# Query products cut into steps of two and three matmuls, and the order behind the state product drawn anew

## The chip, the core and the metric

The kernel runs on one NeuronCore of a Trainium2 chip. The metric is the device time of one execution in microseconds (us); less is better. Five engines work from queues of their own, each strictly in the order in which its instructions were issued: TensorE (PE: matmuls, transposes as matmuls, and its weight loads, PEld), VectorE (DVE), ScalarE (ACT), GpSimd (POOL) and SyncE (SP, which only issues transfers here). Semaphores carry the waits between them.

## The reference

The kernel computes a transformer block on 2048 tokens of 640 features: linear attention with 32 heads of 20 features and softmax feature maps, then a two-layer SiLU network of 1728 hidden units, each behind a layer norm and with a residual.

```python
qkv = layernorm(x) @ wqkv;  q, k, v = heads(qkv)        # 32 heads of 20
pq, pk = q @ w_phi[h], k @ w_phi[h]
phi_q = concat(softmax(pq), softmax(-pq));  phi_k likewise
kv = phi_k.T @ v;  z = phi_k.sum(tokens)                # the state, per head
o  = (phi_q @ kv) / (phi_q @ z + 1e-6)
h  = x + o @ wo
out = h + silu(layernorm(h) @ w1) @ w2
```

## The kernel before

The 2048 tokens are 16 tiles of 128 (number t in what follows). The order of all instructions is written out by hand: a string `ORDER` holds words such as `dp.1@2`, and a loop calls the function `op_dp(1)` with PSUM bank 2. PSUM has eight banks of 128 x 512 fp32, and the digits behind `@` say which bank, or the first of which banks, the step writes. The loop stands in a manual schedule, so that each engine gets its instructions in the order of the words; only the waits between engines (a bank that is still read, a tile that isn't yet written) are put in by the framework.

Start. `lx`, `lk`, `lv`, `lo`, `l1`, `l2`, `lh` load x, the key and value weights, the output weights and the two network weights. `wm` are matmuls of constants on PE, of 512, 256 or 128 columns. `wt.c` transposes the key weights chunk by chunk, `wc.c` copies the chunk out, `fk.c` multiplies it with the block-diagonal w_phi (`ph` builds that on DVE) and `fc.c` copies the folded weights out; `gk`, `gc` do the same for the query weights. `st`, `rs` and `xn.t` normalise x; `xt`/`xc` (on PE) or `xd` (a transposing transfer) transpose it.

Keys and values. `kp.t` and `vp.t` are ten matmuls of 320 columns each, `ke.t` takes the two exponentials on ACT, `kr.t` the softmax sums and their reciprocals on DVE, `kn.t` scales the exponentials (L411 on POOL, L415 on DVE; the letter behind it says which of the 64 rows of 20 go to POOL: `p` all, `b` 32, `q` 48), `vc.t` copies the values out. `cc.t` adds tile t into the state, which lies in bank 7. `kc` and `km` (ACT, then DVE) bring the finished state into the form that the next stage needs.

Queries and attention. `qp.g.i` is the query product for token group g (four tiles) and feature part i (L455): parts 0 and 1 are two banks with five matmuls of 512 columns each, part 2 one bank with five. `qe.g.i` takes the exponentials with two activations on ACT (L465). `dp.t` multiplies the queries of tile t with the state (L490): forty small matmuls into four banks. `dw.t` (L508, L509, L511, L514) combines the two halves on DVE and so empties the four banks; `dr.t` takes the reciprocal, `do.t` divides (on POOL, or on DVE with `v`), `td.t` is a transposing transfer and `op.t` the output projection, ten matmuls of 320 columns (L552). `oa.t` adds it to x on DVE.

Network. `sq`, `sr`, `hn` are the second layer norm, `hd` its transposing transfer; `up.g.k` and `ua.g.k` the first layer with SiLU (L631, L641, L653), `yp.t.half` and `yh` the second (L677, L690), `yo` and `yz` the residual and the store. The five groups here are tiles 0-1, 2-5, 6-9, 10-13 and 14-15.

Two waits matter in what follows. A step that writes a bank waits until the bank's last reader is done, so `dp` waits for the `dw` of the tile that had its banks, and a product that takes a bank from `qp` waits for `qe`. And a `dp` that waits holds back all that stands behind it on PE.

Of the kernel before, what the change touches and what calls it, by code (L numbers as in the profile page):

```python
# [9 lines left out]
ALU = mybir.AluOpType  # L10
# [29 lines left out]
vp.15@4 gk.0@0 gc.0.a kn.10.p kr.8 kn.8.p vc.15.a kp.14@2 ke.14 kr.14 kn.14.p l1.0.s xd.7 vp.7@0 kp.7@4  # L40
# [16 lines left out]
yo.3 sr.9 hn.9.v hd.9 dr.15 do.15.1.v hd.8 yp.2.0 dr.14 hn.7.a sq.11 sr.11 hn.10.a yp.5.1 hd.7 sr.13 yp.4.0
yo.5 do.14.1.v hn.13.a yp.4.1 up.2.2@6 ua.2.2 up.2.5@4 ua.2.5 hn.11.v hd.11 up.2.3@6 up.2.0@4 do.15.0.v
ua.2.0 yo.2 hd.13 hd.10 up.3.1@0 up.2.4@4 ua.2.4 ua.3.1 yo.4 up.3.0@2 ua.3.0 ua.2.3 up.3.4@4 ua.3.4 up.2.6@0
ua.2.6 up.3.3@2 ua.3.3 up.2.1@6 td.15 op.15@4 oa.15 do.14.0.p td.14 op.14@0 ua.2.1 yp.7.0@2 oa.14 sq.14  # L60
up.3.6@6 sr.14 yh.2.1@4 yp.7.1 yo.7 yp.9.1 up.3.2@0 ua.3.2 yp.9.0 sq.15 sr.15 hn.15.v yp.6.1@2 yp.6.0
yp.8.0@0 ua.3.6 yp.8.1 up.3.5@6 ua.3.5 yo.9 yp.10.0@4 hn.14.a hd.14 hd.15 yh.2.0 yo.6 yh.3.0@6 yp.10.1 yo.10
yp.12.1 yp.11.1@2 yp.12.0 up.4.2@4 ua.4.2 yo.8 up.4.1@0 ua.4.1 yo.12 up.4.3@6 up.4.0@4 ua.4.0 yp.11.0
yh.3.1@0,1 yo.11 ua.4.3 yh.4.0@4,6 yp.15.0 yp.15.1 yo.15 yp.14.1 yp.14.0 yp.13.0 yo.14 yz.13.0.s yp.13.1
yz.13.1.a
"""

@with_exitstack
def kernel(
# [86 lines left out]
    Wfq = persist.tile([P, C, D], BF16, name="Wfq")  # L156
# [5 lines left out]
    tl = {}  # L162
    XnT, EqT, HnT, shT = {}, {}, {}, {}
# [243 lines left out]
    def op_kn(t, split="p"):  # L407
        Ek3 = tl["ek", t][:].rearrange("p s (h f) -> p (s h) f", f=DH)
        Sk = tl["sk", t]
        n = {"p": 2 * H, "q": 48, "b": H}[split]  # L410
        nc.gpsimd.tensor_tensor(  # L411
            Ek3[:, 0:n], Ek3[:, 0:n], Sk[:, 0:n].unsqueeze(2).to_broadcast([P, n, DH]), op=ALU.mult,
        )
        if n < 2 * H:
            nc.vector.tensor_tensor(  # L415
                Ek3[:, n:], Ek3[:, n:], Sk[:, n:].unsqueeze(2).to_broadcast([P, 2 * H - n, DH]), op=ALU.mult,
            )
# [30 lines left out]

    QR = [(0, 1), (2, 3), (4,)]

    def op_qp(g, i):
        ps = mm2() if len(QR[i]) == 2 else mm1().unsqueeze(1)
        for k, r in enumerate(QR[i]):
            for c in range(C):
                nc.tensor.matmul(  # L455
                    ps[:, k, :], Wfq[:, c, r * P : (r + 1) * P], XnT[g][:, c, :],
                    start=(c == 0), stop=(c == C - 1),
                )
        tl["qp", g, i] = ps
# [284 lines left out]
```

## Time and profile before

| | |
|---|---|
| median of three runs | 238.02 us (237.96 to 238.08) |
| the profiled execution, its own time | 238.42 us |
| its span, first to last instruction | 236.6 us |
| PE / DVE / ACT / POOL busy | 97% / 56% / 50% / 40% |
| transfers | 20.67 MB, 87 GB/s on average |
| last matmul ends | 233.83 us into the span |

Times in the views are microseconds from the start of the span. A row of the timeline gives start, length, engine, line of the kernel, operation, tiles and shapes, and the count of instructions that were merged; in brackets stands how long the engine was idle ahead of it and what ended that. A few matmul records are missing from the trace. Matmuls overlap in the pipeline, so the length of a row has the drain of its last matmul in it, and the next row often starts before the row ahead has ended.

### The profile page before, as it was taken

Reading aid. Unit: us, or ns where it says so; the run is one execution under the profiler, and the core shown is the slowest. Engines: PE = TensorE matmul, PEld = TensorE weight load, DVE = VectorE, ACT = ScalarE, POOL = GpSimd, SP = SyncE. Lnnn points to the kernel's source line nnn. Section 1 sums busy time; section 2 is a strip of 40 time slices with the busy share of each in tenths; the row PEclk is TensorE's granted clock in tenths of the full one; section 3 lists DMA queues with packets and bytes.
Section 4 is the critical chain, followed back from the end, with each engine's and each line's share of the span. In section 5 each row is a group of like instructions: output and inputs, shape, how many; then the busy total and the mean of one; then the engine's idle time right before and its main releaser. Section 6 shows DMA issues by size and latency. Waiting matters only on the chain.

```text
span 236.6 us, 6282 instructions
## 1 busy us (share of the span) xinstructions
PE 229.5 (97%) x2651; PEld 148.4 (63%) x2672; DVE 133.0 (56%) x250; ACT 117.6 (50%) x175; POOL 94.7 (40%) x187
## 2 busy tenths in 40 slices
PE   8999999999998999999999999999999999999995
PEld 4767777776554455876655576754446667578762
DVE  3999998997858989769785467240002101121122
ACT  3979999878676575755142473412463140303200
POOL 7437889999923543845023057600000310000000
PEclk9999999999999999999999999999999999999999
DMA  7988766990001199464347400654000000040011
GB/s 208 340 310 119 83 146 130 160 261 7 3 3 30 28 194 187 53 150 83 93 38 79 77 0 19 128 127 95 0 3 0 0 28 30 14 124 30 11 47 55
DMA packets 44844, 20.67 MB, mean 87 GB/s; under 512 B 34448, under 2 KB 44304, under 8 KB 44816
## 3 DMA queue, kind: packets, MB, share of 16 engines
q1 hardware_dynamic: 43728, 19.88, 39.1%
q10 hardware_dynamic: 1088, 0.39, 0.7%
q8 instruction: 21, 0.34, 0.7%
q14 instruction: 7, 0.06, 0.1%
HBM read 9.61 MB, written 2.62 MB: 52 GB/s over the span
## 4 chain that ended last, share of the span: by engine, by line
PE 86%; DMA 5%; DVE 4%; ACT 2%; issue 1%; SPq 1%; DVEq 0%; ACTq 0%
PE mm L677 24%; PE mm L631 22%; PE mm L368 17%; PE mm L552 8%; PE mm L455 7%; DMA wv<-in_A_wqkv_dram 3%; PE mm L490 2%; PE mm L424 2%; DMA X<-in_A_x_dram 1%; PE mm L641 1%; PE mm L690 1%; DVE u L511 1%; DVE u L514 1%; ACT EqT L465 1%; ACT sq L569 1%
## 5 line engine op out<-in xcount | busy, mean ns | idle before, releaser
L653 ACT ACTIVATE shT<-mm 128x1024 bf16<-128x1024 f32 (+2 forms) x29 | 27.5, 962 | 64.4 <-PE mm L631 55.8
L631 PE MATMUL mm<-HnT,w 128*128 128x512 bf16 (+1 forms) x315 | 58.1, 335 | 0.9 <-ACT shT L653 0.2
L677 PE MATMUL mm<-w,shT 128*128 128x320 bf16 (+2 forms) x415 | 58.3, 299 | 0.1
L677 PEld LDWEIGHTS <-shT 128*128 128x128 bf16 x416 | 39.7, 98 | 17.6 <-issue 1.3
L631 PEld LDWEIGHTS <-w 128*128 128x128 bf16 x325 | 31.4, 98 | 23.3 <-issue 0.4
L368 PEld LDWEIGHTS <-XnT 128*128 128x128 bf16 x320 | 30.8, 98 | 12.7 <-issue 0.8
L411 POOL TENSOR_TENSOR Ek<-Ek,Sk 128x1280 bf16<-128x1280 bf16 (+1 forms) x16 | 35.7, 2266 | 1.0 <-DVE Sk L404 1.0
L698 DVE TENSOR_TENSOR ob<-mm,X 128x640 bf16<-128x640 f32 x15 | 12.2, 823 | 40.6 <-PE mm L690 19.3
L561 DVE SCALAR_TENSOR_TENSOR X<-mm,X 128x640 bf16<-128x640 f32 x16 | 13.1, 819 | 29.1 <-PE mm L552 29.1
L525 POOL TENSOR_TENSOR o<-u,rd 128x320 bf16<-128x320 f32 x21 | 15.9, 778 | 23.5 <-DVE rd L519 15.9
L465 ACT ACTIVATE EqT<-mm 128x1024 bf16<-128x1024 f32 (+1 forms) x24 | 19.6, 884 | 10.2 <-PE mm L455 10.1
L368 PE MATMUL mm<-wv,XnT 128*128 128x320 bf16 x160 | 24.0, 299 | 0.4 <-DMA wv<-in_A_wqkv_dram 0.3
L401 DVE TENSOR_REDUCE Sk<-Ek 128x64 f32<-128x1280 bf16 x16 | 23.2, 1448 | 1.8 <-ACT Ek L393 1.8
L368 PE MATMUL mm<-Wfk,XnT 128*128 128x320 bf16 x160 | 23.9, 299 | 0.0
L552 PE MATMUL mm<-wo,ot 128*128 128x320 bf16 x160 | 23.6, 299 | 0.2 <-ACT EqT L465 0.2
L455 PE MATMUL mm<-XnT,Wfq 128*128 128x512 bf16 x90 | 21.9, 379 | 1.2 <-issue 0.9
L393 ACT ACTIVATE Ek<-mm 128x640 bf16<-128x640 f32 x32 | 20.5, 717 | 3.7 <-PE mm L368 3.6
L574 POOL TENSOR_SCALAR hm<-hst 128x1 f32<-128x1 f32 x16 | 3.2, 198 | 47.2 <-DVE X L561 47.2
L552 PEld LDWEIGHTS <-ot 128*128 128x128 bf16 x160 | 15.3, 98 | 7.2 <-issue 0.7
L569 ACT ACTIVATE sq<-X 128x640 bf16<-128x640 bf16 x16 | 11.7, 734 | 11.1 <-DVE X L561 9.4
L271 DVE BATCH_NORM_STATS2 stats<-X 128x6 f32<-128x320 bf16 x32 | 13.7, 470 | 4.2 <-DMA X<-in_A_x_dram 4.1
L455 PEld LDWEIGHTS <-Wfq 128*128 128x128 bf16 x100 | 9.1, 98 | 9.7
(77 smaller groups left out, 217.4 us busy)
## 6 DMA issues: line engine op xcount, KB each, us to landing
out_dram<-ob SPq DMA_DIRECT2D x15, 160.0 KB, 1.8
w<-in_B_w_dram SPq DMA_DIRECT2D x6, 360.0 KB, 3.9
X<-in_A_x_dram SPq DMA_DIRECT2D x3, 640.0 KB, 9.4
w<-in_B_w_dram SPq DMA_DIRECT2D x5, 320.0 KB, 3.4
wk<-in_A_wqkv_dram SPq DMA_DIRECT2D x4, 160.0 KB, 3.7
wv<-in_A_wqkv_dram SPq DMA_DIRECT2D x1, 480.0 KB, 7.9
wo<-in_A_wo_dram SPq DMA_DIRECT2D x1, 480.0 KB, 11.9
w<-in_B_w_dram SPq DMA_DIRECT2D x1, 480.0 KB, 5.1
```

Source lines behind the costliest of these rows:

```text
L368: nc.tensor.matmul(ps[:, half, 0:320], tok(XnT[t // GT], t)[:, c, :], W[:, c, half * 320 : (half + 1) * 320], start=(c == 0), stop=(c == C ...
L393: nc.scalar.activation(Ek[:, s, :].rearrange("p (a n) -> p a n", a=2), tl["kp", t][:, :, 0:320], AF.Exp, scale=1.0 - 2.0 * s,)
L401: nc.vector.tensor_reduce(Sk[:], tl["ek", t][:].rearrange("p s (h f) -> p (s h) f", f=DH), axis=AX.X, op=ALU.add,)
L411: nc.gpsimd.tensor_tensor(Ek3[:, 0:n], Ek3[:, 0:n], Sk[:, 0:n].unsqueeze(2).to_broadcast([P, n, DH]), op=ALU.mult,)
L455: nc.tensor.matmul(ps[:, k, :], Wfq[:, c, r * P : (r + 1) * P], XnT[g][:, c, :], start=(c == 0), stop=(c == C - 1),)
L465: nc.scalar.activation(E[:, s, rs[0] : rs[-1] + 1, :], tl["qp", g, i][:, 0 : len(rs), :], AF.Exp, scale=1.0 - 2.0 * s,)
L525: (nc.vector if eng == "v" else nc.gpsimd).tensor_tensor(tl["o", t][:, a * 320 : (a + 1) * 320].rearrange("p (h f) -> p h f", f=DH), tl["u ...
L552: nc.tensor.matmul(ps[:, half, 0:320], tl["ot", t][:, c, :], wo[:, c, half * 320 : (half + 1) * 320], start=(c == 0), stop=(c == C - 1),)
L569: nc.scalar.activation(sq[:], X[:, t, :], AF.Square, accum_out=tl["hst", t][:, 1:2])
L631: nc.tensor.matmul(ps[:, i * W : (i + 1) * W], w1[:, c, fc * P : (fc + 1) * P], HnT[g][:, c, 0:W], start=(c == 0), stop=(c == C - 1), skip ...
L653: nc.scalar.activation(sh[:, a:b], tl["up", g, k][:, 0 : b - a], AF.Silu)
L677: nc.tensor.matmul(ps, shT[g][:, fc * W + i * P : fc * W + (i + 1) * P], w2[:, fc, a:b], start=first and fc == 0, stop=last and fc == FC - ...
```

## The change

Five things change; the amount of matrix work doesn't, but for the `wm`.

1. `op_qp` issues only the first two matmuls of a part's first bank. The three others are a word of their own, `qs`, and the second bank has `qr` (two) and `qt` (three). `qe` follows when all are issued.
2. The order around and behind the state product is written anew with these smaller words. `dp` now mostly stands behind the first two matmuls of the next part, or between `qr` and `qt` of one, and it takes banks 0 to 3 (only `dp.14` takes 4 to 7), where before its banks changed.
3. `kn` has two more splits, `d` (16 rows on POOL, 48 on DVE) and `v` (all on DVE); tiles 2, 5, 6, 7 and 10 use `d`, `q`, `q`, `v` and `d`. `vc.7` and `vc.12` go from ACT to DVE, `xn.2` from DVE to ACT, and eight halves of `do` from DVE to POOL, one the other way; `hn` of seven tiles changes between ACT and DVE.
4. Ahead of the first transpose `wt.0` stand seven `wm` of 512 columns, not nine and one of 256; behind it come four of 256 and one of 128, not one of each.
5. Weight loads move: `l1.2`, `l2.4.6` and `l2.6.8` come ahead of the attention stage, `l2.8.10` goes behind its start.

```diff
-mk mo lx.0.1.a st.0 rs.0.1 lk.0.1.s lp.a ph.v wm.512@7 wm.512@7 wm.512@7 wm.512@7 wm.512@7 wm.512@7 wm.512@7
-wm.512@7 wm.512@7 wm.256@7 wt.0@0 lx.1.2.s lk.4.5.a lk.1.2.s wm.256@2 wm.128@2 wt.1@1 st.1 lk.2.3.s lk.3.4.s
+mk mo lx.0.1.a lk.0.1.s lp.a lx.1.2.s lk.4.5.a wm.512@7 wm.512@7 wm.512@7 wm.512@7 wm.512@7 wm.512@7
+wm.512@7 wt.0@0 lk.1.2.s ta wc.0.a wm.256@2 wm.256@2 wm.256@2 wm.256@2 wm.128@2 wt.1@1 wc.1.a st.0 rs.0.1
...
-vc.7.a ke.7 qp.0.1@2 kr.15 qe.0.1 cc.6 cc.10 kr.7 cc.13 cc.8 kn.15.p qp.0.0@0 qe.0.0 vp.14@4 vc.14.a
-qp.0.2@6 l2.2.4.s kn.7.b cc.15 cc.7 qe.0.2 mc.1 mt cc.14 kc km.0 l1.5.s km.1 qp.3.0@2 dp.0@4 qe.3.0 qp.2.0@0
-qe.2.0 close dw.0.p dr.0 do.0.0.p do.0.1.p dp.1@2 qp.1.0@6 dw.1.p dr.1 do.1.0.p dp.3@0 dw.3.p dr.3 qe.1.0
-do.3.0.p qp.1.1@4 qe.1.1 td.0 do.3.1.p dp.2@0 dw.2.p dr.2 qp.1.2@6 qe.1.2 do.1.1.p td.1 op.0@4 oa.0 l2.6.8.s
...
-td.4 hn.1.v oa.2 dp.9@0 dw.9.p sq.2 sr.2 hn.2.a td.3 op.3@4 oa.3 sq.3 op.4@6 l1.2.s hd.0 hd.1 dr.5 do.5.1.p
...
+kn.8.p kn.10.d vp.15@4 vc.15.a kp.15@0 ke.15 kp.14@2 gk.0@4 gc.0.a vp.7@0 ke.14 kr.14 kn.14.p qp.0.1@4
+qs.0.1 qr.0.1 kp.7@2 ke.7 l2.10.13.s kr.15 l1.2.s cc.8 vc.7.v cc.13 l2.2.4.s cc.10 qt.0.1 qp.0.0@2 qs.0.0
+kn.15.p qr.0.0 qt.0.0 qe.0.1 l2.4.6.s kr.7 kn.7.v l2.6.8.s qe.0.0 vp.14@0 vc.14.a qp.0.2@6 qs.0.2 cc.6 cc.7
+mt qe.0.2 cc.15 cc.14 kc km.0 lh.s qp.3.0@4 qs.3.0 qr.3.0 km.1 dp.0@0 l1.4.s close dw.0.p dr.0 qt.3.0
+do.0.1.p qe.3.0 qp.2.0@6 qs.2.0 qr.2.0 qt.2.0 qe.2.0 do.0.0.p dp.1@0 dw.1.p qp.1.0@4 dr.1 do.1.0.p qs.1.0
+qr.1.0 qt.1.0 qe.1.0 qp.1.1@6 td.0 do.1.1.p td.1 dp.3@0 dw.3.p dr.3 do.3.0.p qs.1.1 qr.1.1 qt.1.1 qe.1.1
+qp.3.2@4 qp.1.2@5 dp.2@0 dw.2.p qs.1.2 qe.1.2 do.3.1.p td.3 qs.3.2 op.0@6 dr.2 do.2.1.p do.2.0.p qe.3.2 oa.0
+dp.4@0 dw.4.p td.2 sq.0 qp.2.2@5 qs.2.2 qe.2.2 op.1@6 oa.1 sr.0 qp.2.1@4 dp.6@0 dw.6.p l1.5.s l1.1.s qs.2.1
+qr.2.1 hn.0.a hd.0 sq.1 qt.2.1 sr.1 hn.1.v hd.1 qe.2.1 op.3@6 oa.3 sq.3 dp.5@0 dw.5.p op.2@4 sr.3 oa.2
+hn.3.a sq.2 dr.5 do.5.0.p do.5.1.p qp.3.1@6 qs.3.1 l2.0.2.s l2.8.10.s qr.3.1 dp.9@0 dw.9.p td.5 dr.9
+do.9.0.p dr.6 do.6.1.p dr.4 do.4.1.p do.4.0.p td.4 qt.3.1 qe.3.1 up.0.2@4 ua.0.2 dp.7@0 sr.2 up.0.0@6 ua.0.0
+dw.7.p dr.7 up.0.3@4 ua.0.3 do.6.0.p dp.8@0 dw.8.p dr.8 hn.2.a up.0.1@6 ua.0.1 td.6 do.8.0.p op.5@4 oa.5
...
-        n = {"p": 2 * H, "q": 48, "b": H}[split]
+        n = {"p": 2 * H, "q": 48, "b": H, "d": 16, "v": 0}[split]
...
+    def qcut(g, i, k, cs):
+        r = QR[i][k]
+        for c in cs:
+            nc.tensor.matmul(
+                tl["qp", g, i][:, k, :], Wfq[:, c, r * P : (r + 1) * P], XnT[g][:, c, :],
+                start=(c == 0), stop=(c == C - 1),
+            )
+
     def op_qp(g, i):
...
+        tl["qp", g, i] = mm2() if len(QR[i]) == 2 else mm1().unsqueeze(1)
+        qcut(g, i, 0, range(2))
+
+    def op_qs(g, i):
+        qcut(g, i, 0, range(2, C))
+
+    def op_qr(g, i):
+        qcut(g, i, 1, range(2))
+
+    def op_qt(g, i):
+        qcut(g, i, 1, range(2, C))
```

More of the change, by code (lines that the diff above doesn't have):

```diff
@@ new lines @@
+dp.12@0 dw.12.p dr.12 yp.1.0@6 do.7.1.p do.7.0.p sq.5 td.7 hd.3 op.4@4 oa.4 sr.5 hn.5.v hd.5 do.9.1.p sq.4
+td.9 sr.4 hn.4.a dp.10@0 dw.10.p yp.1.1 yp.0.1@4 yh.0.0 hd.2 hd.4 yo.1 dp.11@0 dw.11.p dr.11 do.8.1.p
+do.11.0.p td.8 yp.0.0 yo.0 op.7@6 oa.7 sq.7 dr.10 op.6@0 oa.6 sq.6 sr.6 op.9@2 up.1.6@4 do.11.1.v td.11 oa.9
+sq.9 dp.15@0 ua.1.6 sr.9 up.1.5@6 ua.1.5 up.1.1@4 hn.9.v hd.9 do.10.0.p dw.15.p dr.15 hn.6.v hd.6 op.8@6
+oa.8 sq.8 op.11@0 ua.1.1 sr.7 hn.7.v hd.7 up.1.3@2 oa.11 do.12.1.p sr.8 hn.8.v do.15.0.p dp.14@4 dw.14.p
@@ new lines @@
+dr.14 do.14.0.v hd.8 ua.1.3 up.1.4@0 ua.1.4 do.14.1.v td.14 up.1.0@2 sq.11 sr.11 hn.11.v ua.1.0 up.2.6@4
+ua.2.6 dp.13@0 dw.13.p dr.13 do.13.1.p up.2.0@6 up.2.5@4 ua.2.5 op.14@0 up.1.2@2 ua.2.0 oa.14 sq.14 up.2.2@4
+ua.1.2 do.12.0.p td.12 sr.14 op.12@6 oa.12 ua.2.2 hn.14.v do.10.1.p do.15.1.v yp.4.0@0 up.2.4@2 ua.2.4 td.10
+op.10@4 oa.10 up.2.1@6 sq.12 sr.12 hn.12.a hd.11 hd.12 up.2.3@2 ua.2.1 yp.2.0@4 ua.2.3 yp.9.0@6 do.13.0.p
+td.13 hd.14 yh.2.1@2 td.15 yh.1.0 yp.2.1 yo.2 yp.9.1 yo.9 op.13@4 yp.4.1 yo.4 sq.10 sr.10 yp.6.0@6 op.15@0
@@ new lines @@
+hn.10.v hd.10 oa.15 sq.15 sr.15 oa.13 hn.15.a hd.15 yp.7.1 yp.7.0 yo.7 yp.3.0@0 yp.5.0@4 yh.1.1 yh.2.0@2
+sq.13 sr.13 yp.6.1 yo.6 yp.3.1 yp.5.1 yo.5 hn.13.v up.4.1@6 hd.13 up.4.2@4 yp.8.1 yp.8.0 ua.4.2 yo.3
+up.3.0@0 ua.3.0 yo.8 up.3.3@2 ua.3.3 up.3.5@4 ua.3.5 up.4.0@0 ua.4.0 up.3.1@2 ua.3.1 ua.4.1 up.3.2@4 ua.3.2
+up.4.3@0 ua.4.3 yp.14.0@2 yp.15.0@6 up.3.4@4 up.3.6@0 yh.4.0 yp.15.1 ua.3.4 ua.3.6 yp.11.0@4 yp.12.1@0 yo.15
+yp.14.1 yo.14 yp.10.1@6 yh.3.1@2,3 yh.3.0 yp.10.0 yo.10 yp.12.0 yo.12 yp.11.1 yo.11 yp.13.0 yz.13.0.s
@@ L66 @@
+yp.13.1 yz.13.1.a
 """
@@ L293, in op_xn @@
         xn = first.tile([P, D], BF16, name="xn", bufs=7)
-        if eng == "v":
-            nc.vector.tensor_scalar(
+        if eng != "a":
+            (nc.vector if eng == "v" else nc.gpsimd).tensor_scalar(
                 out=xn[:], in0=X[:, t, :], scalar1=mv[:, 0:1], scalar2=rstd[:, 0:1],
@@ L449 @@
     QR = [(0, 1), (2, 3), (4,)]
-    def op_qp(g, i):
[L452 to L459, printed above, removed]
+    def qcut(g, i, k, cs):
[4 more added lines that the diff above has]
+                start=(c == 0), stop=(c == C - 1),
+            )
+    def op_qp(g, i):
+        tl["qp", g, i] = mm2() if len(QR[i]) == 2 else mm1().unsqueeze(1)
[6 more added lines that the diff above has]
+        qcut(g, i, 1, range(2, C))
     def op_qe(g, i):
```

51 lines of the change are left out of this document (15 added, 36 removed).

## The prediction

> **What bounds the kernel now.** I read the page first, then the waits of PE, then PE's timeline, where I measured each hole from the starts of the matmuls.
>
> ```profile
> span 236.6 us, 6282 instructions
> PE 229.5 (97%) x2651; PEld 148.4 (63%) x2672; DVE 133.0 (56%) x250; ACT 117.6 (50%) x175; POOL 94.7 (40%) x187
> ...
> PE mm L490 <- DVE u L514: 0.8, 3, 0.3
> PE mm L368 <- DMA wv<-in_A_wqkv_dram: 0.3, 1, 0.3
> PE mm L552 <- ACT EqT L465: 0.2, 1, 0.2
> ```
>
> PE is the bound, and the change leaves its matmuls as they are, but for the warm-ups. So only holes can be won, and the waits name few. They count from the modelled end of a matmul; counted from starts the holes are wider. Here is PE from the first attention product on:
>
> ```profile
> 68.94 0.47 PE L490 MATMUL mm<-KVBD,EqT 32*128 32x44 bf16 x40
> 69.57 2.10 PE L455 MATMUL mm<-XnT,Wfq 128*128 128x512 bf16 x9 [0.16 <-issue]
> 71.61 0.19 PE L490 MATMUL mm<-KVBD,EqT 32*128 32x44 bf16 x2
> 72.09 0.45 PE L490 MATMUL mm<-KVBD,EqT 32*128 32x44 bf16 x38 [0.29 <-DVE u L514]
> 72.70 2.11 PE L455 MATMUL mm<-XnT,Wfq 128*128 128x512 bf16 x9 [0.16 <-issue]
> 74.74 0.19 PE L490 MATMUL mm<-KVBD,EqT 32*128 32x44 bf16 x2
> 75.11 0.45 PE L490 MATMUL mm<-KVBD,EqT 32*128 32x44 bf16 x38 [0.17 <-DVE u L514]
> 75.71 2.11 PE L455 MATMUL mm<-XnT,Wfq 128*128 128x512 bf16 x9 [0.16 <-issue]
> 78.13 0.46 PE L490 MATMUL mm<-KVBD,EqT 32*128 32x44 bf16 x40 [0.31 <-DVE u L514]
> 78.52 1.25 PE L455 MATMUL mm<-XnT,Wfq 128*128 128x512 bf16 x4
> 79.85 1.52 PE L552 MATMUL mm<-wo,ot 128*128 128x320 bf16 x10
> ...
> L455 PEld LDWEIGHTS <-Wfq x100: 95/98/99, 57.6 to 91.5; 128*128 128x128 bf16 x100
> L455 PE MATMUL mm<-XnT,Wfq x90: 379/379/390, 57.7 to 91.7; 128*128 128x512 bf16 x90
> ```
>
> Nine records of ten: 100 weight loads but 90 query matmuls, so each row of nine lacks one, and the "issue" ahead of it is that matmul. Its spacing is (2.11 - 0.379) / 8 = 0.216 us. Now the holes. dp.1: its first matmuls start at 71.61, the others at 72.09: 0.47. dp.3: 74.74 to 75.11: 0.36. dp.2: dp.1 and dp.3 start 0.07 ahead of the end of the query row (69.57 + 2.10 = 71.67 and 74.81), so dp.2 would at 77.75 and does at 78.13: 0.38. op.0: the row ahead ends at 79.77, and an output product starts 0.16 ahead of that where nothing holds it: 79.61 against 79.85, 0.24.
>
> ```profile
> 92.42 1.53 PE L552 MATMUL mm<-wo,ot 128*128 128x320 bf16 x10
> 94.12 1.52 PE L552 MATMUL mm<-wo,ot 128*128 128x320 bf16 x10 [0.16 <-ACT EqT L465]
> 95.57 0.47 PE L490 MATMUL mm<-KVBD,EqT 32*128 32x44 bf16 x40
> 95.97 4.54 PE L631 MATMUL mm<-HnT,w 128*128 128x256 bf16 x40
> 100.44 0.47 PE L490 MATMUL mm<-KVBD,EqT 32*128 32x44 bf16 x40
> 101.14 1.03 PE L631 MATMUL mm<-HnT,w 128*128 128x256 bf16 x8 [0.23 <-ACT shT L653]
> ```
>
> op.4: due at 93.95 - 0.16 = 93.79, starts at 94.12: 0.33. up.0.1: behind dp.7 the next product starts 0.07 ahead of the row's end (96.04 and 95.97), so due at 100.84, it starts at 101.14: 0.30. Together 0.47 + 0.36 + 0.38 + 0.24 + 0.33 + 0.30 = **2.08 us**. That is what the redrawn stretch can give at most.
>
> **The change part by part.** *The loop of dp and dw.* A dp writes four banks, dw empties them, the next dp of those banks waits:
>
> ```profile
> 67.90 0.58 DVE L442 TENSOR_TENSOR KVBD<-KVF,maskS 128x315 bf16<-128x315 bf16 x2
> 75.71 0.36 DVE L508 RECIPROCAL w<-mm 128x32 f32<-128x32 f32 x1 [0.27 <-PE mm L490]
> 77.22 0.85 DVE L514 TENSOR_TENSOR u<-u,mm 128x672 f32<-128x672 f32 x1
> ```
>
> dp.3's last matmuls end at 75.56, DVE starts at 75.71 and ends at 78.07, dp.2 starts at 78.13. A dp of 0.46 and this make 0.46 + 0.15 + 2.36 + 0.06 = 3.03 from one start to the next in the same banks (2.97 where DVE starts 0.09 behind the dp, as after 78.59). PE's time between two dps is today ten query matmuls: 0.41 (dp's own: 68.94 to 69.57 less the one lost record) + 10 x 0.216 + 0.09 for the change to small matmuls = 2.66. The turn is longer than that, so PE stands. In the new order 13, 12 and 12 query matmuls stand between dp.0, dp.1, dp.3 and dp.2: 3.31, 3.09 and 3.09. The three holes go (1.21), with 0.06 to 0.12 to spare twice. Behind dp.2 it is six matmuls and op.0 (0.41 + 1.30 + 1.36 + 0.09 = 3.16), behind dp.4 five and op.1, with `oa.1` ahead of dw.6 on DVE, about 0.1 to spare. These margins are about as wide as what I can read, so I charge 0.10 for the four together (bounds 0 and 0.4).
>
> *op.0 and op.4.* op.0 takes bank 6 now, which qe.1.1 leaves with over 12 matmuls and a dp in between; op.4 comes far behind qe.3.1. Both holes go (0.57). But op.2@4 comes to stand where op.4 stood: a query part, an output product, a dp, then op.2 in that part's banks. The same items in another sequence, behind the same two activations, so the same **0.33** (bounds 0.2 and 0.4).
>
> *up.0.1* waits in both orders for the SiLU activation that empties its bank. Today ACT comes to that late, with only dp.8 behind up.0.0 to cover it; in the new order up.0.3 and dp.8 do, and ACT begins with up.0.2 earlier against PE. I charge 0.05 (bounds 0 and 0.30, the hole of today).
>
> *dp.0.* Seven query matmuls, not ten, stand between the last cc and dp.0: it is due 3 x 0.216 earlier, at 68.29. KVBD is ready at 68.48, and 0.06 later dp.0 can start: a new hole of **0.25** (bounds 0.15 and 0.35).
>
> *Ahead of the state.* The key scaling moves between POOL and DVE:
>
> ```profile
> L411 POOL TENSOR_TENSOR Ek<-Ek,Sk 128x640 bf16<-128x640 bf16 x3 | 4.9, 1658 | 0.0
> L415 DVE TENSOR_TENSOR Ek<-Ek,Sk 128x640 bf16<-128x640 bf16 x3 | 4.1, 1380 | 0.1
> 56.67 2.35 POOL L411 TENSOR_TENSOR Ek<-Ek,Sk 128x1280 bf16<-128x1280 bf16 x1
> 59.99 1.20 PE L424 MATMUL mm<-Ek,Vp 128*21 128x40 bf16 x128
> 50.00:57.00 7.00, 7.00 (x128) 5.28 (x117) 5.65 (x7) 5.64 (x11) 7.00 (x4) 1.00 0.52 118
> 57.00:66.00 9.00, 8.89 (x196) 5.04 (x200) 7.13 (x7) 6.02 (x9) 8.93 (x6) 1.00 0.02 4
> ```
>
> In the last two rows (a window, its length, then PE, PEld, DVE, ACT and POOL busy) POOL is full, and DVE has 1.35 and 1.87 us free. For tiles 2, 5, 6, 7 and 10 POOL had 2.35 x 2 + 1.66 x 3 = 9.7 us; it gets 2 x 16 + 2 x 48 = 128 rows, two whole pieces, 4.7. DVE had 4.1 and gets 192 rows against 96: 8.3 at the same price, 4.2 more, and `vc.7` and `vc.12` beside, some 0.85 each by L514's row, the nearest with as many elements out of PSUM; it gives `xn.2` to ACT, where it ends ahead of 13.49. PE needs this in time for the cc steps: kn.8, done at 59.02 today, is now asked for by the first cc of its group, three query matmuls earlier than today's first: 59.99 - 0.65 = 59.34. On POOL it no longer has kn.10's whole piece ahead of it. So POOL, full until now, gets 5 us of room, and DVE loses what it had. I take 0 (bounds 0 and 2.7, rivals).
>
> *Start.* Two and a half of ten warm-ups go, about 1 us:
>
> ```profile
> 4.84 0.74 PE L320 MATMUL mm<-ident,wk 128*128 128x128 bf16 x5
> 6.69 0.44 PE L320 MATMUL mm<-ident,wk 128*128 128x128 bf16 x5
> ...
> 13.49 0.70 PE L368 MATMUL mm<-wv,XnT 128*128 128x320 bf16 x4 [0.32 <-DMA wv<-in_A_wqkv_dram]
> 5.19 8.26 DMA wv<-in_A_wqkv_dram
> ```
>
> It comes to nothing. From 13.49 on PE depends on the value weights, which land 8.26 us behind an issue on SP at 5.19, and SP's issues ahead of that are the same ones in the same order. If that cover were gone, the microsecond would show. The bounds are 0 and 0.9 late (rivals).
>
> *The rest.* Behind 101 PE has hardly a hole before, so nothing is to be won; the moved weight loads leave SP's queue ahead of the transposes freer, and the moved `do` and `hn` end far ahead of the products that need them. I take 0 (bounds -0.2 and +0.5). The last product and both stores are the same.
>
> Sum: -2.08 + 0.10 + 0.33 + 0.05 + 0.25 = **-1.35 us**. The profiled execution took 238.42 around its span of 236.6; less 1.35 that is 237.07. The median of the runs is 0.40 below that execution, so **236.7 us** (236.67).
>
> **Rivals.** *DVE makes the state late (slower).* DVE's added 4.2 + 1.7 = 5.9 us against 1.35 + 1.87 = 3.2 free: the state, and all behind it, would come 2.7 later: 239.4. It decides where the overflow passes 1.35 + 0.48 = 1.8. Against it speak these rows, kn.7's half on DVE and what POOL did beside it:
>
> ```profile
> 62.66 1.67 DVE L415 TENSOR_TENSOR Ek<-Ek,Sk 128x640 bf16<-128x640 bf16 x1
> 61.30 2.36 POOL L411 TENSOR_TENSOR Ek<-Ek,Sk 128x1280 bf16<-128x1280 bf16 x1
> 63.61 1.86 POOL L411 TENSOR_TENSOR Ek<-Ek,Sk 128x640 bf16<-128x640 bf16 x1
> ```
>
> DVE's 1.67 us end 0.67 behind POOL's row (63.66), as if it had waited for that; and POOL's next half took 1.86, 0.68 above a half of 2.36. They look like taking turns, so a half on DVE would be 0.67 of work and the rest waiting. At that price the added 96 rows are 2.0, the whole 3.7 against 3.2 free, and POOL's lighter load shortens the waits. For it speaks that nothing in the trace shows a kn mostly on DVE. Chance 0.14.
>
> *The margins of the dp loop don't hold.* Nearly all dps now share banks 0 to 3. If each of fourteen turns stands 0.1, the gain is given back: 238.1. For it: 0.06 to spare is less than the spread of DVE's start (0.09 to 0.15). Against it: behind dp.2 output and network products stand between. Chance 0.08.
>
> *PE stays slow at the start.* The same five transposes take 0.74 us at 4.84 and 0.44 at 6.69: I read that as a lower clock at first, though the page's clock row doesn't resolve it. If with fewer warm-ups it lasted over four more such groups, at 0.30 each, PE would come 1.2 later to 13.49, less the 0.32 that it waits there: 0.9 lost, 237.6. Against it: between the first transpose and the second, new warm-ups fill PE. Chance 0.04. The Trainium skill ("TensorE: Matmul & The Clock Gate", What's actually happening) says that PE's clock is released by a window of about 3.4 us in which PE was busy, and that this window runs freely. By that rule fewer warm-ups are a risk only where they leave PE idle; this trace has one change of pace, between 4.84 and 6.69.
>
> That the change doesn't do what it says is no case of its own: cutting `qp` alone moves nothing, and all that I count hangs on where dp stands.
>
> **How the numbers follow.** Forecast (about -1.35, holes as summed) 0.74; state late 0.14; margins 0.08; slow clock 0.04. The forecast is faster by over 0.2% (0.48 us, about what a measurement of this kernel tells from no change), 0.74; the margins and the slow clock are within it, 0.12; the late state is slower, 0.14. Low end: all six holes gone, nothing but op.2's 0.2 back, and 0.2 in the rest: 238.02 - 2.1 = 235.9. High end: the margins (238.1) and the small overflows of the late state, 238.3. Outside lie about 0.06 below and 0.12 above.
>
> **What would show it.** Right: no wait of the dps on L514 ahead of 80 us, one of about 0.25 on KVBD ahead of the first dp, one of about 0.3 of L552 on ACT's L465 near 88, and the first of the value products still waiting for wv until 13.5. Wrong: PE waiting for L411 or L415 ahead of cc, L490 waiting for L514 in many places, or transposes of 0.7 us behind 6.

## The result, and the profile after

| | before | after |
|---|---|---|
| median of six runs | 238.05 us (237.96 to 238.49) | 236.57 us (235.99 to 237.22) |
| the profiled execution | 238.42 us | 236.78 us |
| its span | 236.6 us | 234.8 us |

The ratio of the times is 0.9936, 95% interval 0.9918 to 0.9954: 1.5 us faster, and outside the 0.2% that a measurement of this kernel can tell from nothing. The forecast was 236.7, with 235.9 to 238.3.

In the changed file the lines lie a little further down: the small products `dp` are L504 (L490 before), the last step of `dw` L528 (L514), the query products L457 (L455), their exponentials L479 (L465), the output products L566 (L552), the network's first layer L645 (L631), the state products `cc` L427 (L424) and the key scaling L414 on POOL and L418 on DVE (L411, L415). The head of the page, and below it the waits of PE (line waited for: us in total, times, longest):

```profile
span 234.8 us, 6284 instructions
PE 228.1 (97%) x2653; PEld 148.0 (63%) x2672; DVE 133.4 (57%) x249; ACT 114.6 (49%) x171; POOL 95.4 (41%) x190
```

```profile
...
PE mm L322 <- DMA wk<-in_A_wqkv_dram: 0.5, 1, 0.5
PE mm L645 <- issue: 0.3, 2, 0.2
PE mm L370 <- DMA wv<-in_A_wqkv_dram: 0.3, 1, 0.3
PE mm L566 <- ACT EqT L479: 0.3, 1, 0.3
PE mm L427 <- issue: 0.2, 1, 0.2
```

The wait of the small products for DVE, three times and 0.8 us in all, is gone from the list. One wait for the exponentials on ACT is left. PE's timeline, as in the prediction (start, length, engine, line; in brackets the idle time ahead):

```profile
66.91 1.46 PE L457 MATMUL mm<-XnT,Wfq 128*128 128x512 bf16 x6 [0.16 <-issue]
68.30 0.49 PE L504 MATMUL mm<-KVBD,EqT 32*128 32x44 bf16 x40
68.72 2.98 PE L457 MATMUL mm<-XnT,Wfq 128*128 128x512 bf16 x12
71.63 0.47 PE L504 MATMUL mm<-KVBD,EqT 32*128 32x44 bf16 x40
72.03 2.76 PE L457 MATMUL mm<-XnT,Wfq 128*128 128x512 bf16 x11
74.73 0.46 PE L504 MATMUL mm<-KVBD,EqT 32*128 32x44 bf16 x40
75.35 2.54 PE L457 MATMUL mm<-XnT,Wfq 128*128 128x512 bf16 x11 [0.16 <-issue]
77.82 0.47 PE L504 MATMUL mm<-KVBD,EqT 32*128 32x44 bf16 x40
...
83.82 0.59 PE L457 MATMUL mm<-XnT,Wfq 128*128 128x512 bf16 x2
84.39 0.46 PE L504 MATMUL mm<-KVBD,EqT 32*128 32x44 bf16 x40
...
87.97 0.47 PE L504 MATMUL mm<-KVBD,EqT 32*128 32x44 bf16 x40
88.71 1.52 PE L566 MATMUL mm<-wo,ot 128*128 128x320 bf16 x10 [0.27 <-ACT EqT L479]
...
98.64 0.47 PE L504 MATMUL mm<-KVBD,EqT 32*128 32x44 bf16 x40
99.03 2.36 PE L645 MATMUL mm<-HnT,w 128*128 128x256 bf16 x20
```

The turns of the small products are 3.33, 3.10 and 3.09 us (68.30, 71.63, 74.73, 77.82), where 3.31, 3.09 and 3.09 were forecast; each starts 0.07 ahead of the end of the row before it, as one that nothing holds does. The last row pair is `up.0.1`: 0.39 from the start of the small product to the next start, no hole.

How the 1.8 us come about: the first small product starts at 68.30 against 68.94, but has three query matmuls fewer in front of it (3 x 0.216 = 0.65), so up to there nothing is won or lost. All of it comes behind: the last product but one starts at 228.56 against 230.35, 1.78 earlier.

### The profile page after: what moved, and what is told of

It reads as the page before. It is cut to its first block, busy times and chain, and to the rows that moved or that the text cites. A ratio compares the mean times of both kernels' runs of the same rounds, so it can differ in the third digit from the quotient of the medians.

```text
span 234.8 us, 6284 instructions
## 1 busy us (share of the span) xinstructions
PE 228.1 (97%) x2653; PEld 148.0 (63%) x2672; DVE 133.4 (57%) x249; ACT 114.6 (49%) x171; POOL 95.4 (41%) x190
## 4 chain that ended last, share of the span: by engine, by line
PE 91%; DMA 5%; issue 1%; ACT 1%; DVE 0%; ACTq 0%; SPq 0%
PE mm L691 24%; PE mm L645 24%; PE mm L370 17%; PE mm L457 9%; PE mm L566 9%; DMA wv<-in_A_wqkv_dram 3%; PE mm L504 3%; PE mm L427 2%; DMA phr<-in_A_w_phi_dram 2%; PE mm L655 1%; PE mm L704 1%; ACT EqT L479 1%; PE mm L337 1%; DVE ob L721 0%; PE mm L308 0%
## 5 line engine op out<-in xcount | busy, mean ns | idle before, releaser
L645 PE MATMUL mm<-HnT,w 128*128 128x512 bf16 (+1 forms) x317 | 57.5, 335 | 0.6 <-issue 0.3
L645 PEld LDWEIGHTS <-w 128*128 128x128 bf16 x325 | 31.4, 98 | 23.3
L414 POOL TENSOR_TENSOR Ek<-Ek,Sk 128x1280 bf16<-128x1280 bf16 (+2 forms) x15 | 32.9, 2217 | 4.1 <-DVE Sk L406 4.1
L539 POOL TENSOR_TENSOR o<-u,rd 128x320 bf16<-128x320 f32 x28 | 19.9, 727 | 23.0 <-DVE rd L533 16.4
L566 PE MATMUL mm<-wo,ot 128*128 128x320 bf16 x160 | 23.9, 299 | 0.3 <-ACT EqT L479 0.3
L457 PE MATMUL mm<-XnT,Wfq 128*128 128x512 bf16 x90 | 22.1, 379 | 1.2 <-issue 1.0
L479 ACT ACTIVATE EqT<-mm 128x1024 bf16<-128x1024 f32 (+1 forms) x24 | 19.7, 879 | 4.9 <-PE mm L457 4.8
L566 PEld LDWEIGHTS <-ot 128*128 128x128 bf16 x160 | 15.7, 98 | 7.3 <-issue 0.2
L457 PEld LDWEIGHTS <-Wfq 128*128 128x128 bf16 x100 | 9.0, 98 | 9.3
L525 DVE TENSOR_TENSOR u<-mm,w 128x672 f32<-128x672 f32 x16 | 13.7, 858 | 1.2 <-DVE w L523 0.3
```

The lines of the kernel that those rows point to most:

```text
L414: nc.gpsimd.tensor_tensor(Ek3[:, 0:n], Ek3[:, 0:n], Sk[:, 0:n].unsqueeze(2).to_broadcast([P, n, DH]), op=ALU.mult,)
L457: nc.tensor.matmul(tl["qp", g, i][:, k, :], Wfq[:, c, r * P : (r + 1) * P], XnT[g][:, c, :], start=(c == 0), stop=(c == C - 1),)
L479: nc.scalar.activation(E[:, s, rs[0] : rs[-1] + 1, :], tl["qp", g, i][:, 0 : len(rs), :], AF.Exp, scale=1.0 - 2.0 * s,)
L525: nc.vector.tensor_tensor(u[:], A[1][:, :, :, 0:21], w[:].unsqueeze(3).to_broadcast([P, 4, 8, 21]), op=ALU.mult,)
L539: (nc.vector if eng == "v" else nc.gpsimd).tensor_tensor(tl["o", t][:, a * 320 : (a + 1) * 320].rearrange("p (h f) -> p h f", f=DH), tl["u ...
L566: nc.tensor.matmul(ps[:, half, 0:320], tl["ot", t][:, c, :], wo[:, c, half * 320 : (half + 1) * 320], start=(c == 0), stop=(c == C - 1),)
```

## The experiments

Twelve runs on two chips, each beside the kernel before; between runs of different chips the ratios compare better than the times. In some files the order's text is shorter or a function is added; there L501 stands for L504 and L424 for L427 (three lines less), and L511 and L573 for L504 and L566 (seven more).

**The changed kernel again, twice.** No edit.

> The changed kernel once more, unedited, as the base for the other kernels on the same chip. Its six times lay between 235.99 and 237.22 us, 1.23 apart, against 0.53 for the kernel before. If the spread belongs to this order, it shows again here, with a median between 236.3 and 236.8 and a second profile whose holes on PE are in the same places (0.35 ahead of the product behind the fifth small product, none ahead of the small products). If it was chance, the times lie within 0.5 us.

> The changed kernel unedited, beside the run above on the same chip: 236.6 us (236.4 to 236.8), in the profile the wait for L479 near 88 us, and at 50 us a stop of 0 to 0.4 us that is there when the load of PE's instructions ends later than about 48.4 us.

Measured: 236.58 us (236.03 to 236.97), ratio 0.993 (0.9915 to 0.9945), and 236.70 (236.37 to 237.81), ratio 0.9948 (0.9929 to 0.9967). Beside the first the kernel before spread as widely (237.61 to 238.77 in 22 runs), beside the second less (237.69 to 238.64 in 11); that the spread belongs to the new order is not shown. Both profiles have the wait for the exponentials near 88 us and none of the small products for DVE. The first of the two profiles has a span of 234.3: there the value products do not wait for their weights (0.30 us in the profile shown above), and PE doesn't stop in the state products at 50 us, where it stood 0.38 us above and 0.45 us in the second. (A stop is counted from the start of one matmul to the start of the next.) It costs less than its length: from the first start to the last end the 160 matmuls take 1.80 and 1.88 us with these two stops and 1.62 without. That stop is the matter of four of the runs below.

**Whole query parts around the first four small products.**

```diff
-qp.3.0 qs.3.0 qr.3.0 km.1 dp.0 .. qt.3.0        qp.1.1 .. dp.3 .. qs.1.1        qp.3.2 qp.1.2 dp.2 qs.1.2 .. qs.3.2
+qp.3.0 qs.3.0 qr.3.0 qt.3.0 km.1 dp.0 ..        dp.3 .. qp.1.1 qs.1.1           dp.2 qp.1.2 qs.1.2 .. qp.3.2 qs.3.2
```

> The changed kernel with the first four small products (tiles 0, 1, 3, 2) again between whole query parts, ten matmuls apart; all else stays. Theory (the gain is the turn of the small products: 3.03 us from start to start in the same banks, while ten query matmuls make 2.66): PE stands 0.37 ahead of each of three small products, waiting for L528, and the kernel takes 1.1 us more than the changed one, 237.7 (237.4 to 238.0). Rival (the gain comes from the scaling's new splits and the new start; where the small products stand is of no weight): the same time as the changed kernel, within 0.3 us.

Measured: 237.67 us, ratio 0.9976 (0.9966 to 0.9987), 1.09 above the unedited kernel beside it (the first of the two above). PE's timeline of that profile (L525 is the last step of `dw`):

```profile
68.78 0.46 PE L501 MATMUL mm<-KVBD,EqT 32*128 32x44 bf16 x40
...
72.00 0.46 PE L501 MATMUL mm<-KVBD,EqT 32*128 32x44 bf16 x40 [0.49 <-DVE u L525]
...
74.96 0.46 PE L501 MATMUL mm<-KVBD,EqT 32*128 32x44 bf16 x40 [0.24 <-DVE u L525]
...
77.92 0.46 PE L501 MATMUL mm<-KVBD,EqT 32*128 32x44 bf16 x40 [0.24 <-DVE u L525]
```

The three waits are back, and seven tenths of the gain (1.09 of 1.54) are gone with nothing else undone. So it is the place of these steps that pays. The price was right in sum and not for each turn: counted from starts, the holes are 0.55, 0.31 and 0.30 us (1.16), where 0.37 each was expected. The last two turns are 2.96 us; the first is 3.22, because DVE pauses 0.28 us between two of its steps there, in which semaphore instructions of 0.05 us each stand. The same pause stands in the first turn of the kernel before (0.21) and of the changed one (0.28), where 13 matmuls (3.33) cover it.

**Only the first small product moved, in the kernel before.** (The other query products are spelled in the new words, in the old order.)

```diff
-qp.3.0@2 qs.3.0 qr.3.0 qt.3.0 dp.0@4
+qp.3.0@2 qs.3.0 qr.3.0 dp.0@4 qt.3.0
```

> The kernel before with one thing changed: the small product of tile 0 stands three matmuls earlier, ahead of the last three of its neighbour's query part. Theory: it starts at about 68.3 us, once the first half of KVBD is there, the turn to the next small product is 3.31 us and no longer too short, so the hole of 0.47 us there goes, while those of 0.36 and 0.38 behind stay; 0.4 us less than before, 237.6 to 237.8. The working of the prediction, by which all of KVBD must be there (68.54), gives 0.2 less. Rival (the earlier finish of one turn moves the same wait to the next): the same time as before.

Measured: 237.72 us, ratio 0.9978 (0.9964 to 0.9991), 0.49 less than before; by the interval 0.2 to 0.9, so the time alone does not tell the expected 0.4 from 0.2. The profiled execution was the slowest of the twelve (238.66): PE waited 1.4 us for the key weights at its start, and all comes some 0.6 us later than expected. DVE's row of KVBD and PE's timeline:

```profile
68.48 0.57 DVE L445 TENSOR_TENSOR KVBD<-KVF,maskS 128x315 bf16<-128x315 bf16 x2
```

```profile
68.87 0.55 PE L504 MATMUL mm<-KVBD,EqT 32*128 32x44 bf16 x40
...
72.27 0.47 PE L504 MATMUL mm<-KVBD,EqT 32*128 32x44 bf16 x40
...
75.31 0.45 PE L504 MATMUL mm<-KVBD,EqT 32*128 32x44 bf16 x38 [0.18 <-DVE u L528]
...
78.32 0.46 PE L504 MATMUL mm<-KVBD,EqT 32*128 32x44 bf16 x40 [0.30 <-DVE u L528]
```

The hole ahead of the second small product is gone, those ahead of the third and fourth stay: one turn made longer wins its own hole and hands nothing on. The rows also tell when a small product may start. KVBD is written in two halves, the first done at 68.81 (0.335 after its start), the second at 69.05; PE starts at 68.87, 0.18 ahead of the end of the second. Its row is 0.55 long in place of 0.47: the wait for the second half falls inside it.

**The old splits of the key scaling, with the old value copies, and each alone.**

```diff
-kn.2.d kn.5.q kn.6.q kn.7.v kn.10.d   vc.7.v vc.12.v
+kn.2.b kn.5.b kn.6.p kn.7.b kn.10.p   vc.7.a vc.12.a     first run: all;  second: kn alone;  third: vc.12 alone
```

> The changed kernel with the key scaling of tiles 2, 5, 6, 7, 10 split between POOL and DVE as in the kernel before, and the value copies of tiles 7 and 12 on ACT again; all else stays. Theory (the new splits are needed, as cover, by the earlier state product): POOL gets some 3.5 us more between 43 and 66 us against 1.9 us in which it stands there, so the last scalings end about 1.3 us too late, PE waits for L414 ahead of the state product, and the kernel takes 1.3 us more than the changed one (0.5 to 2.0). Rival (the splits are worth nothing, as the prediction's zero for them says read strictly): within 0.3 us of the changed kernel.

> The changed kernel with the key scaling of tiles 2, 5, 6, 7 and 10 split as before; the value copies stay as in the changed kernel. With the copies put back too, 0.87 us were lost, and that profile shows two lates at once: PE stands 1.0 us in the middle of the state products at 50 us, and POOL ends its last scaling at 66.7 us, when PE comes to it 0.9 us late anyway. Theory A (POOL): without the stop at 50 us PE comes to the scaling of tile 7 at 65.8 and waits for POOL until 66.7; the kernel takes 0.8 us more than the changed one (0.5 to 1.1). Theory B (the stop at 50 us is the whole loss, and it hangs on the value copy): as fast as the changed kernel, within 0.3 us.

> The changed kernel with the value copy of tile 12 on ACT again; all else stays. On ACT it stands ahead of the normalisation of tile 15, which ended 1.3 us later in the profile with the copies put back; behind that come the transposing transfers and the network weights, and PE stood 1.0 us in the state products at 50 us while no engine that it needed was late. Theory B (the late transfers cause the stop): the stop of 0.6 to 1.0 us is there, and the kernel takes 0.4 to 0.9 us more than the changed one. Theory A (the loss was POOL's; the stop is chance): within 0.3 us of the changed kernel, with a stop of 0.4 us or less.

Measured: all, 237.45 us, ratio 0.9969 (0.9958 to 0.9979); splits alone, 237.21, 0.9955 (0.9939 to 0.9972); the copy alone, 237.60, 0.9969 (0.9955 to 0.9983). The unedited kernel has 0.9930 and 0.9948: the medians are 0.5 to 1.0 us above it, and the losses do not add. The intervals of "all" and of the copy alone lie above that of the first unedited run (to 0.9945) and overlap with the second's (to 0.9967); that of the splits alone overlaps with both, so there the waits below are the better evidence. PE's waits and timeline with the splits alone:

```profile
PE mm L427 <- POOL Ek L414: 0.7, 2, 0.4
```

```profile
59.98 0.38 PE L427 MATMUL mm<-Ek,Vp 128*21 128x40 bf16 x32 [0.24 <-POOL Ek L414]
...
66.42 0.93 PE L427 MATMUL mm<-Ek,Vp 128*21 128x40 bf16 x96 [0.41 <-POOL Ek L414]
```

With the old splits PE is idle for POOL by 0.24 and 0.41 us. Counted by the ends of the two groups it is more, 0.35 and 0.51 (59.08 + 0.93 = 60.01 against 60.36; 65.64 + 1.20 = 66.84 against 67.35), near the 0.8 expected. The new splits are cover that the new order needs. The copy alone loses in another place, where no engine is late (state products at 50 us):

```profile
49.10 1.05 PE L427 MATMUL mm<-Ek,Vp 128*21 128x40 bf16 x108
51.54 0.56 PE L427 MATMUL mm<-Ek,Vp 128*21 128x40 bf16 x52 [1.39 <-issue]
```

With both put back, this stop (1.0 us there) brought PE so late to the scaling at 66 us that POOL's delay hardly showed: two lates side by side cost little more than the longer one. The wait for POOL that was expected of that run did not come, only its loss. Both theories held, each for its own edit, but the copy's stop (1.57) and loss (1.0) were larger than the 1.0 and 0.9 expected at most.

**Two loads of network weights moved.** In the trace the queue of instruction loads (16 KB each) shows one load ahead of each stop, and PE goes on 1.2 to 1.5 us behind its end:

| kernel | load of instructions | PE goes on | stop |
|---|---|---|---|
| changed, first profile | 47.49 to 48.63 | 50.13 | 0.38 |
| changed, second repetition | 47.43 to 48.60 | 49.89 | 0.45 |
| changed, old warm-ups (below) | 47.52 to 48.63 | 49.85 | 0.24 |
| all old splits and copies | 48.46 to 49.59 | 50.95 | 1.02 |
| copy alone | 48.97 to 50.13 | 51.54 | 1.57 |
| changed, first repetition | 46.78 to 47.94 | no stop | 0.1 |

```diff
 copy alone, and:
-xn.7.a l1.3.s kn.6.q ..  cc.5 l1.0.s ke.10 ..  km.0 lh.s qp.3.0
+xn.7.a kn.6.q ..         cc.5 ke.10 ..         km.0 lh.s l1.3.s l1.0.s qp.3.0
```

> The kernel with the value copy of tile 12 on ACT again, which stood 1.6 us in the state products at 50 us and took about 0.95 us more than the changed kernel; here two loads of network weights (l1.3 and l1.0) are moved from SP's queue at 40 to 44 us to behind the state, at 67 us. In six profiles the load of PE's own instructions ends within 0.25 us of the end of the stream of data transfers behind those weights, and PE goes on 1.2 to 1.5 us behind it. Theory (PE stops because its instructions come late behind the weights): with the weights gone the load of instructions starts earlier, the stop is gone (all 160 products in one row of at most 1.7 us), and the time is that of the changed kernel, within 0.3 us. Rival (the stop belongs to the late copy or the late normalisation, whatever the weights do): the stop of 1 us or more stays, and so does the time of 237.6.

Measured: 236.67 us (236.42 to 236.99), ratio 0.9932 (0.9917 to 0.9947): the loss of the copy is gone. (One reading in the expectation is off: it is the start of the load, not its end, that lies within 0.3 us of the end of the stream, 47.49 against 47.74 in the first profile, 48.97 against 49.18 with the copy alone.) The transfers from 45.0 to 49.5 us in 40 slices of 0.1125 us, busy tenths and GB/s, first with the copy alone, then with the weights moved:

```profile
DMA  9999999999570000899999499999999999990000
GB/s 317 323 318 284 294 268 246 166 112 82 43 30 20 20 20 18 125 279 320 290 266 210 92 333 333 328 333 333 293 280 298 289 291 55 210 192 18 0 0 0
...
q8 instruction: 1, 0.02, 1.6%
```

```profile
DMA  9999400000600000000000000000000000000000
GB/s 216 200 223 185 82 7 0 0 0 0 146 0 0 0 0 0 0 0 0 0 0 0 0 0 0 0 0 0 0 0 0 0 0 0 0 0 0 0 0 0
...
q8 instruction: 1, 0.02, 1.7%
```

The lone 146 GB/s is the load itself (16,384 bytes in 0.1125 us), at 46.20; in the upper view it starts at 48.97, with the last slices of the stream. PE's timeline with the weights moved:

```profile
48.57 1.62 PE L427 MATMUL mm<-Ek,Vp 128*21 128x40 bf16 x160
...
67.79 0.25 PE L504 MATMUL mm<-KVBD,EqT 32*128 32x44 bf16 x10
68.52 0.39 PE L504 MATMUL mm<-KVBD,EqT 32*128 32x44 bf16 x30 [0.47 <-issue]
```

The stop at 50 us is gone, and a smaller one stands inside the first small product: the moved weights keep the transfers busy to 63 us, one load of instructions runs from 62.36 to 63.51 (60.06 to 61.21 in the changed kernel), the next from 66.29 to 67.23 (64.99 to 65.94), and PE goes on 1.29 behind that. So the copy on ACT costs nothing by itself that these runs can see. With all put back, the normalisation of tile 15 behind it starts at 36.46 us in place of 35.19, and the transposing transfers on SP at 37.41 in place of 36.19; the weights stand behind them in that queue, and the stream of transfers ends later.

**The last hole.** The exponentials of part 1 of group 2 by bank; then with the weights behind the state; then with them behind the second transposing transfer of the attention.

```diff
+    def op_qa(g, i, k):
+        E = get(EqT, eqp, g, [P, 2, C, GT * P], "EqT")
+        for s in range(2):
+            nc.scalar.activation(
+                E[:, s, QR[i][k], :], tl["qp", g, i][:, k, :], AF.Exp, scale=1.0 - 2.0 * s,
+            )
...
-sq.1 qt.2.1 sr.1 hn.1.v hd.1 qe.2.1
+sq.1 qa.2.1.0 qt.2.1 sr.1 hn.1.v hd.1 qa.2.1.1
...
-km.0 lh.s qp.3.0                  do.1.1.p td.1 dp.3
+km.0 lh.s l1.3.s l1.0.s qp.3.0    do.1.1.p td.1 dp.3               second run
+km.0 lh.s qp.3.0                  do.1.1.p td.1 l1.3.s l1.0.s dp.3 third run
```

> The changed kernel with the exponentials of query part 1 of group 2 taken by bank, four activations of 512 columns in place of two of 1024, so that the first bank is free before the output product of tile 2 comes to it. Theory (the last hole is this product's wait for both banks, 0.35 us): PE no longer waits for L479 near 88 us, the product starts right behind the fifth small product, and the kernel takes 0.35 us less than the changed one, 236.2 (236.0 to 236.5). Rival (ACT, with four activations of about 0.54 us in place of 1.94 us for two, is late with what stands behind, and a wait of the same length appears there): within 0.15 us of the changed kernel.

> The changed kernel with both edits that took something away: the exponentials of one query part bank by bank (236.24 us alone) and the two loads of network weights behind the state. Theory: the small stop at 50 us, 0.24 and 0.38 us in two of the profiles and absent in the others, goes as well, and the median is 0.1 to 0.2 us below that of the exponentials alone, 236.1 (235.8 to 236.3). Rival (the weights now meet the transposing transfers of the first attention outputs, and an output product waits for one): the same as the exponentials alone or more, with a wait of L566's kin for a transfer near 79 us.

> As the kernel with both edits, but the two loads of network weights stand behind the second transposing transfer of the attention outputs, at about 75 us, where PE takes its instructions more slowly (query matmuls of 0.22 us each). Behind the state they had moved the stop from the state products to the first small product (0.46 us at 68 us, 1.3 us behind the end of a load of instructions). Theory: no stop at 50 us and none at 68 us, no new one behind, and 0.4 to 0.6 us less than the unedited changed kernel beside it: 236.1 (235.8 to 236.3). Rival (each place of these weights holds up some load of instructions, or a transposing transfer): no better than the exponentials bank by bank alone, 236.24, or slower, with a stop or a wait for a transfer between 75 and 100 us.

Measured: 236.24 us (236.06 to 236.53), ratio 0.9910 (0.9891 to 0.9928); 236.47, 0.9926 (0.9910 to 0.9942); 236.05, 0.9920 (0.9904 to 0.9937). By bank alone, the first rows are PE's and the last ACT's:

```profile
87.60 0.47 PE L511 MATMUL mm<-KVBD,EqT 32*128 32x44 bf16 x40
87.99 1.53 PE L573 MATMUL mm<-wo,ot 128*128 128x320 bf16 x10
```

```profile
85.93 2.03 ACT L486 ACTIVATE EqT<-mm 128x512 bf16<-128x512 f32 x4
```

The wait is gone; 0.39 from start to start. Four activations take 2.03 us, 0.09 more than two, and begin earlier. The second run missed: the stop at 50 us was gone, but the first small product got one of 0.46 us, as above. In the third neither is there:

```profile
48.60 1.60 PE L427 MATMUL mm<-Ek,Vp 128*21 128x40 bf16 x160
...
67.80 0.49 PE L511 MATMUL mm<-KVBD,EqT 32*128 32x44 bf16 x40
...
87.89 1.53 PE L573 MATMUL mm<-wo,ot 128*128 128x320 bf16 x10
```

It took 236.05 us against 236.70 of the unedited changed kernel beside it and 238.11 of the kernel before; the intervals of the two ratios still touch (0.9937 and 0.9929), so 0.65 us is likely and not certain. Against the exponentials by bank alone nothing is gained: their ratio (0.9910) is no worse than that of the third run (0.9920), and their profile had no stop at 50 us either (0.11). So what the three runs show is the exponentials by bank: the wait is gone from all three profiles, and the first median is 0.34 us lower than that of the unedited kernel on its chip, with intervals that still overlap. That moving the weights adds to it is not shown.

**The old warm-ups in the changed kernel.**

```diff
-wm.512 x7 wt.0 .. wm.256 x4 wm.128 wt.1
+wm.512 x9 wm.256 wt.0 .. wm.256 wm.128 wt.1
```

> The changed kernel with the warm-ups of the kernel before around the first transpose (nine of 512 columns and one of 256 ahead, one of 256 and one of 128 behind it); all else stays. Theory (hidden: PE waits for the second chunk of the key weights until 5.98 us and for the value weights until 13.4 us in any case): the same time within 0.3 us, the second group of transposes starts at about 6.0 us at full pace. Rival (fewer warm-ups keep PE slow for longer, and the new start cost part of the gain): faster than the changed kernel by 0.3 to 0.9 us. A third reading is that the spread of the changed kernel's times comes from its start: then this one's times lie within 0.5 us.

Measured: 236.74 us (236.47 to 237.21), ratio 0.9939 (0.9926 to 0.9952), 0.16 above the unedited kernel beside it, whose ratio of 0.9930 lies inside the interval. The number of warm-ups is worth nothing that these runs can see. The times lie 0.74 apart, so the third reading falls too. One detail missed: the second group of transposes starts at 5.69 us, not 6.0, and at half pace until 6.0.

## Why the prediction was right, and where not

| term | forecast | measured in the profiled execution |
|---|---|---|
| six holes | -2.08 | all gone |
| margins of four small products | +0.10 | +0.05: `dp.6` due 83.82 + 0.59 - 0.07 = 84.34, starts 84.39; none at the others |
| op.2 behind the exponentials | +0.33 | +0.35: due 87.97 + 0.39, starts 88.71 |
| up.0.1 | +0.05 | 0 |
| first small product and KVBD | +0.25 | +0.02 |
| state stage, start | 0 | 0.00 up to the first small product |
| all behind | 0 (-0.2 to +0.5) | -0.12, the rest of the -1.78 |
| sum | -1.35 | -1.78 |

**The mechanism held.** The holes were read from the starts of the matmuls, and their sum, less the new holes, was what the stretch gave. For three of the six (1.21 of the 2.08 us) the run with whole parts shows that they pay and not another part of the change (+1.09 of forecast 1.1), and the run with one step moved shows one of them from the other side (-0.49 of forecast -0.4). That the holes at op.0, op.4 and up.0.1 paid is read from the timeline and was not undone by a run of its own; nor were the moved halves of `do` and `hn`.

**The step that failed is the one at the first small product**: "KVBD is ready at 68.48, and 0.06 later dp.0 can start". KVBD has two halves, and the first twenty of the forty matmuls read only the first. In the changed kernel:

```profile
67.84 0.57 DVE L445 TENSOR_TENSOR KVBD<-KVF,maskS 128x315 bf16<-128x315 bf16 x2
```

The row holds two instructions; the first ends at 68.18, so the small product starts when it is due, at 68.30, and only its second half, which starts at 68.47, 0.06 behind the second instruction's end at 68.41, is 0.02 late. I took the end of a row of two for the time at which its reader may start. The `x2` in the quoted row said so.

**The median hit better than the sum**, and partly by chance. The sum was 0.43 short (0.23 at KVBD, 0.05 each at the margins and at up.0.1, 0.12 behind, which no run explains, less 0.02 at op.2). But the two profiled times differ by 1.64, not 1.78, and the profiled execution of after lay 0.21 above its median, where I had taken 0.40 from before. What an execution lies off its median is not a property to carry over.

**The state stage: a zero that hid something.** PE waited for no scaling, so the zero was right in size, and the slower rival did not come:

```profile
57.00:66.00 9.00, 8.84 (x198) 5.21 (x198) 8.80 (x9) 6.04 (x9) 7.14 (x4) 1.00 0.39 128
```

The columns are the window, its length, then PE, PEld, DVE, ACT and POOL busy. DVE is busy 8.80 of 9.00 us, so it had 0.2 to spare in this window, not the comfort that the prediction had; behind it stand 1.22 us in which DVE waits for ACT's copy of the state. The argument against the rival, that DVE and POOL take turns, is borne out by the scaling of tile 7, now whole on DVE:

```profile
63.75 1.74 DVE L418 TENSOR_TENSOR Ek<-Ek,Sk 128x1280 bf16<-128x1280 bf16 x1
```

```profile
55.68 8.46 POOL L414 TENSOR_TENSOR Ek<-Ek,Sk 128x1280 bf16<-128x1280 bf16 x4 [1.42 <-DVE Sk L406]
```

POOL ends at 64.14; from there DVE needs 1.35 to its end at 65.49, which is twice the 0.67 that the prediction gave for a half. The Trainium skill ("GPSIMD Engine Reference", Specifications) says that the two share their access to SBUF and contend where a DVE instruction has two inputs there; the rows agree. What the prediction did not see is that the new splits are part of the gain, not an aside: without them POOL comes back into PE's path, with 0.65 us of idle time and a median 0.6 us higher.

**The start.** The cover was named rightly for the profiled execution (PE waits for the value weights until 13.36) and four others of the new order; in the rest it was idle there for less than 0.1 us, as the weights had landed earlier. The slow-clock rival did not come, but its reading was too simple: the pace of 128-column matmuls goes from one in 0.107 us to one in 0.056: by 5.0 us in the run with one step moved and near 5.8 in the kernel before, with the same warm-ups, and not before 5.8 in the copy's run with the weights moved, with the new ones. The Trainium skill ("TensorE: Matmul & The Clock Gate", What's actually happening) says that the window runs freely and that the change of pace varies from run to run; the traces agree.

**The margins** of the dp loop held: 0.05 us were lost in one turn.

## What to carry to other kernels

Where an engine's step returns to the same buffers, write down the turn of the one that empties them and the work that stands between on the one that fills them, both from start to start; a hole is the difference, and a few matmuls moved across the step close it without a word of new arithmetic. Look at how many instructions a row merges before taking its end as the time from which a reader may go on. And where PE stands still with no engine late, in a stretch of many small matmuls, look at what the transfers were doing two to three microseconds earlier.

## What the runs showed of the hardware

PE stops in dense stretches of small matmuls (160 of them with their weight loads in 1.62 us) behind a late load of instructions. In seven profiles with such a stop PE went on 1.2 to 1.6 us behind the end of a 16 KB load in the instruction queue, and ahead of the five stops at 50 us the load had started with the end of a stream of data transfers; where the load there ended by 48.43 us, no kernel of the new order stood longer than 0.12 us. Moving 0.7 MB of weights out of the stream took the stop away and put another behind their new place; a third place showed none. That the load holds PE's own instructions is argued, as the trace does not name their engine. But it counts: between the 21 loads of the first profile of the changed kernel PE has 252 rows on average, of 5,340 in all, while DVE, ACT, POOL and SP have 166 to 310 each in the whole run; and all five stops at 50 us stand behind the same matmul, the 108th of the 160.
